# Keeping three more units on chip and loading in tiles twice as long, in a two-pass channel gate

## Chip, cores, metric

The kernel runs on one core of one Trainium2 chip. The metric is device microseconds (us) of one execution. Engines: PE multiplies matrices, DVE works on vectors, ACT applies functions such as the sigmoid, and 16 DMA engines move data between memory (HBM) and the chip's SBUF. PSUM is the small memory that PE adds up in. A packet is the piece of a transfer that the profile records for one DMA engine; here it is one contiguous run of one partition. Ratios are the mean time of one kernel's fast runs over that of the other's fast runs of the same rounds, so they are not quite the ratio of the medians that stand beside them.

## What is computed

Input `x` is 384 x 384 positions of 384 channels in bf16 (113.25 MB). The mean of each channel over all positions goes through a scale and a sigmoid; then every position is multiplied by the result.

```python
g = jnp.einsum("bhwc->bc", x) / (H * W)
s = _sigmoid(g * w1d[0])          # k = 1: cut from the padded sum over k
return x * s[:, None, None, :]
```

The gate needs all of `x` before the first output can be made, and `x` is over four times what the kernel may keep on chip (its budget is 206 KB for each of 128 partitions). So what was not kept has to be read twice.

## The kernel before

`x` is cut into 72 units of 1.573 MB: 128 partitions, 16 consecutive rows (12 KB) each. Pass 1 loads every unit and adds it up on PE, with matmuls against ones into one PSUM tile. The last 13 units stay in SBUF (`res`); the other 59 pass through four slots (`stream`). Pass 2 reads those 59 again, multiplies each in place on DVE and stores it from the ACT queue; then the 13 residents are stored.

```python
# pass 1 (set-up cut)
for t in range(n_tiles):                       # 72
    if t < n_stream:                           # 59
        xt = stream.tile([P, F], mybir.dt.bfloat16, tag="x")
    else:
        xt = res.tile([P, F], mybir.dt.bfloat16, tag="r")
        res_tiles[t] = xt
    nc.sync.dma_start(xt[:], xv[t])
    ...
    for j in range(J):                         # 16 matmuls into acc
        ...
nc.scalar.activation(s_t[:], acc[:], mybir.ActivationFunctionType.Sigmoid, scale=scale_f[:])
# pass 2
for t in range(n_stream):
    xt = stream.tile([P, F], mybir.dt.bfloat16, tag="x")
    nc.sync.dma_start(xt[:], xv[t])
    mul(xt)
    nc.scalar.dma_start(ov[t], xt[:])
for t in range(n_stream, n_tiles):
    xt = res_tiles[t]
    mul(xt)
    nc.scalar.dma_start(ov[t], xt[:])
```

## Time and profile before

| | before |
|---|---|
| time, median of the first 6 runs | 758.73 us (757.11 to 760.18) |
| busy: PE, DVE | 27%, 32% of the span |
| transfers | 131 loads and 72 stores of 1.573 MB |
| DMA rate: pass 1, pass 2, drain | 424, 428, 423 GB/s |

These are lines of the page of the kernel before. DMA and GB/s have one value for each fortieth of the span (a digit is a tenth of busy share). Then come the bytes, the multiply's group, and two DMA issue groups with count, KB each and median us from issue to landing.

```profile
DMA  8999999999999999999999999999999999999899
GB/s 335 424 426 425 423 425 424 426 424 424 426 424 424 425 423 430 427 426 432 422 425 422 429 431 422 422 427 432 425 430 429 431 430 430 432 429 430 373 426 384
...
HBM read 206.05 MB, written 113.25 MB: 422 GB/s over the span
...
L96 DVE TENSOR_TENSOR xt<-xt,s_t 128x6144 bf16<-128x6144 bf16 x72 | 240.3, 3357 | 464.9 <-ACT s_t L91 268.5
...
xt<-in_x_dram SPq DMA_DIRECT2D x131, 1536.0 KB, 12.7
out_dram<-xt ACTq DMA_DIRECT2D x72, 1536.0 KB, 12.9
```

The DMA engines are busy from the second slice to the end and nothing else is: time is bytes over rate, plus holes. One slice near the end (373) and the first and last are lower.

The windows view of the same kernel gives each engine's busy time (count) in a stretch; the last three columns are PE's clock, the DMA share and GB/s. The three rows are pass 1 (reads only), pass 2 (both directions) and the final drain (stores only).

```profile
20.00:260.00 240.00, 179.92 (x1035) 101.37 (x1035) 0.00 (x0) 0.00 (x0) 0.00 (x0) 0.99 1.01 424
300.00:690.00 390.00, 0.00 (x0) 0.00 (x0) 205.46 (x63) 0.00 (x0) 0.00 (x0) 0.50 1.01 428
718.00:752.00 34.00, 0.00 (x0) 0.00 (x0) 0.00 (x0) 0.00 (x0) 0.00 (x0) 0.50 1.00 423
```

The Trainium skill ("DMA: Bandwidth & Descriptors", section "Where 436 GB/s comes from") puts the ceiling of the 16 engines at 435.2 GB/s. This trace is 2 to 3% under it, which fits a ceiling but doesn't yet show one.

Fine windows of the same kernel show the hole near the end. The last streamed unit has been read, its multiply (the third number of a row after the length is DVE) runs, and stores behind it in the ACT queue wait.

```profile
711.00:712.50 1.50, 0.00 (x0) 0.00 (x0) 1.50 (x1) 0.00 (x0) 0.00 (x0) 0.50 0.81 344
712.50:714.00 1.50, 0.00 (x0) 0.00 (x0) 1.50 (x1) 0.00 (x0) 0.00 (x0) 0.50 0.19 82
714.00:715.50 1.50, 0.00 (x0) 0.00 (x0) 0.17 (x1) 0.00 (x0) 0.00 (x0) 0.50 0.35 147
```

At the turn between the passes there is no hole, and the timeline of the same kernel says why. The last matmuls start at 274.06 and the first multiply at 277.47, but loads into the four stream slots were queued long before and keep the engines reading until about 284.

```profile
274.06 2.76 PE L86 MATMUL acc<-xt,ones 128*128 128x384 bf16 x16 [1.98 <-DMA xt<-in_x_dram]
...
276.85 0.58 ACT L91 ACTIVATE s_t<-acc,scale_f 128x384 bf16<-128x384 f32 x1 [267.62 <-PE acc L86]
277.47 22.97 DVE L96 TENSOR_TENSOR xt<-xt,s_t 128x6144 bf16<-128x6144 bf16 x7 [268.48 <-ACT s_t L91]
```

### The profile page before, as it was taken

The page shows a single profiled execution, that of the slowest core. Times are in us where ns is not written, and L with a number is a line of the kernel's source. Part 1 is how long each engine was busy: PE and PEld are TensorE (multiplying, and loading weights), DVE is VectorE, ACT ScalarE, POOL GpSimd, SP SyncE. Part 2 cuts the span into 40 slices and gives each one's busy share as a digit, 9 for nine tenths or more (in the row PEclk, how much of TensorE's full clock was granted, in tenths as well). Part 3 has the DMA queues.
Part 4 walks back from the last instruction along what each step waited for, and adds up shares of the span by engine and source line. Part 5 has one row for each costly group of instructions (what it writes and reads, how often), then busy time and mean ns, then how long its engine had stood idle before and what let it go on. Part 6 is the DMA issues. An engine that isn't in the chain of part 4 may idle for free.

```text
span 757.5 us, 2869 instructions
## 1 busy us (share of the span) xinstructions
PE 202.0 (27%) x1152; PEld 113.5 (15%) x1152; DVE 240.6 (32%) x74; ACT 2.1 (0%) x3; POOL 0.9 (0%) x5
## 2 busy tenths in 40 slices
PE   5687777777777740000000000000000000000000
PEld 2344444444444420000000000000000000000000
DVE  0000000000000038566767563444453544535300
ACT  0000000000000000000000000000000000000000
POOL 0000000000000000000000000000000000000000
PEclk9999999999999985555555555555555555555555
DMA  8999999999999999999999999999999999999899
GB/s 335 424 426 425 423 425 424 426 424 424 426 424 424 425 423 430 427 426 432 422 425 422 429 431 422 422 427 432 425 430 429 431 430 430 432 429 430 373 426 384
DMA packets 29277, 319.48 MB, mean 422 GB/s; under 512 B 3280, under 2 KB 3280, under 8 KB 3280
## 3 DMA queue, kind: packets, MB, share of 16 engines
q1 hardware_dynamic: 18864, 206.05, 64.6%
q10 hardware_dynamic: 10368, 113.25, 35.2%
q8 instruction: 9, 0.15, 0.1%
q14 instruction: 4, 0.03, 0.0%
q0 software_dynamic: 32, 0.00, 0.0%
HBM read 206.05 MB, written 113.25 MB: 422 GB/s over the span
## 4 chain that ended last, share of the span: by engine, by line
DMA 78%; DVE 8%; PE 6%; issue 1%; SPq 0%; DVEq 0%; ACT 0%; POOLq 0%
DMA xt<-in_x_dram 53%; DMA out_dram<-xt 25%; DVE xt L96 8%; PE acc L86 6%; DMA w_b<-in_w1d_dram 1%; SPq L75 0%; DVEq L96 0%; ACT s_t L91 0%; SPq L104 0%; DVE scale_f L79 0%; POOLq L136 0%; POOLq L125 0%
## 5 line engine op out<-in xcount | busy, mean ns | idle before, releaser
L96 DVE TENSOR_TENSOR xt<-xt,s_t 128x6144 bf16<-128x6144 bf16 x72 | 240.3, 3357 | 464.9 <-ACT s_t L91 268.5
L86 PE MATMUL acc<-xt,ones 128*128 128x384 bf16 x1152 | 202.0, 330 | 74.8 <-DMA xt<-in_x_dram 65.8
L86 PEld LDWEIGHTS <-ones 128*128 128x128 bf16 x1152 | 113.5, 99 | 162.9 <-issue 93.0
L79 DVE TENSOR_SCALAR scale_f<-w_b 128x1 f32<-128x1 bf16 x1 | 0.2, 154 | 7.8 <-DMA w_b<-in_w1d_dram 7.8
L91 ACT ACTIVATE s_t<-acc,scale_f 128x384 bf16<-128x384 f32 x1 | 0.6, 581 | 267.6 <-PE acc L86 267.6
L80 ACT ACT_TABLE_LOAD x1 | 1.3, 1283 | 0.7 <-PEq L125 0.7
L78 POOL DMA_DIRECT2D w_b<-in_w1d_dram x1 | 0.7, 661 | 0.8 <-POOLq L125 0.8
L77 DVE MEMSET ones<- 128x128 bf16 x1 | 0.2, 165 | 0.8 <-PEq L125 0.8
L80 ACT ACTIVATE dummy<-scale_f 128x1 f32<-128x1 f32 x1 | 0.2, 204 | 7.0 <-DVE scale_f L79 7.0
L125 POOL MEMSET const-bfloat16-1.0<- 128x1 bf16 x1 | 0.1, 97 | 0.0
L125 POOL MEMSET const-float32-0.0<- 128x1 f32 x1 | 0.1, 94 | 0.2 <-issue 0.2
L125 POOL MEMSET const-float32-1.0<- 128x1 f32 x1 | 0.1, 94 | 0.0
L125 POOL MEMSET const-uint8-127<- 128x1 uint8 x1 | 0.1, 94 | 0.0
## 6 DMA issues: line engine op xcount, KB each, us to landing
xt<-in_x_dram SPq DMA_DIRECT2D x131, 1536.0 KB, 12.7
out_dram<-xt ACTq DMA_DIRECT2D x72, 1536.0 KB, 12.9
w_b<-in_w1d_dram POOLq DMA_DIRECT2D x1, 0.2 KB, 7.6
```

Of the source, the lines that this page charges most:

```text
L77: nc.vector.memset(ones[:], 1.0)
L78: nc.gpsimd.dma_start(w_b[:], w1d.to_broadcast((P, 1)))
L79: nc.vector.tensor_scalar_mul(scale_f[:], w_b[:], 1.0 / float(HW))
L80: nc.scalar.activation(dummy[:], scale_f[:], mybir.ActivationFunctionType.Sigmoid)
L86: nc.tensor.matmul(acc[:], lhsT=ones[:], rhs=xt[:, j * C:(j + 1) * C], start=first, stop=last,)
L91: nc.scalar.activation(s_t[:], acc[:], mybir.ActivationFunctionType.Sigmoid, scale=scale_f[:])
L96: nc.vector.tensor_mul(xt[:].rearrange("p (j c) -> p j c", j=J), xt[:].rearrange("p (j c) -> p j c", j=J), s_bc,)
L125: nc = _bacc.Bacc("TRN2", target_bir_lowering=False, num_devices=1)
```

## The change

The intent is to read three units less in pass 2, to move pass 1 in longer pieces, and to close the hole near the end:

- Two units ("kept") stay in two of the four stream slots between the passes. A third is copied by DVE into six idle PSUM banks as 32-bit words; its product is made from PSUM and stored last but one of the streamed units.
- Pass 1 loads two units at a time as 32 rows (24 KB) per partition, through six slots that later hold 12 of the 13 residents.
- Pass 2 begins with the kept units, the very first in halves, so that stores start early.

```diff
-    for t in range(n_tiles):
-        ...                                    # one unit per load, stream or res slot
+    # ---- pass 1: everything in 32-row tiles through the slots of the later residents
+    for u in range(0, N_RE - 1, 2):            # N_RE = 57
+        bt = bigs.tile([P, 2 * F], mybir.dt.bfloat16, tag="b")
+        nc.sync.dma_start(bt[:], big(xf, u))   # units u, u+1 as 32 rows per partition
+        add_up(bt, 2 * J)
+    # one unit that is read again, then the kept ones, in stream slots
+    xt = stream.tile([P, F], mybir.dt.bfloat16, tag="x")
+    nc.sync.dma_start(xt[:], xv[N_RE - 1])
+    add_up(xt, J)
+    for b in range(F // BK):                   # 6 PSUM banks
+        nc.vector.tensor_copy(keep[b][:], xt[:, b * BK:(b + 1) * BK].bitcast(mybir.dt.float32))
+    for u in range(N_RE, N_RE + KEPT):         # KEPT = 2, in stream slots
+        ...
+    for u in range(N_RE + KEPT, U - 1, 2):     # 6 big residents
+        ...
+    rt = one.tile([P, F], mybir.dt.bfloat16)   # the 13th resident, one unit
+    nc.sync.dma_start(rt[:], xv[U - 1])
+    add_up(rt, J)
     nc.scalar.activation(s_t[:], acc[:], ...Sigmoid, scale=scale_f[:])
+    for a in range(0, 1280, C):                # s_x: the gate repeated, for the PSUM banks
+        ...
+    for n, (u, xt) in enumerate(kept):
+        for a, rows in (((0, J // 2), (J // 2, J // 2)) if n == 0 else ((0, J),)):
+            mul(xt, a, rows)
+            nc.scalar.dma_start(...)
-    for t in range(n_stream):
+    order = list(range(N_RE - 2)) + [N_RE - 1, N_RE - 2]   # the unit in PSUM last but one
+    for u in order:
         ...
+        if u == N_RE - 1:
+            for b in range(F // BK):
+                nc.vector.tensor_mul(xt[:, ...], keep[b][:].bitcast(mybir.dt.bfloat16), s_x[:, o:o + BK])
```

More of the change, by code (lines that the diff above doesn't have):

```diff
@@ L6 @@
 from concourse._compat import with_exitstack
-J_TARGET = 16
-STREAM_BUFS = 4
-SBUF_BUDGET_KB = 206.0
-MIN_TILES_PER_PASS = 4
-def _plan(HW, C, P, jt=None, sbufs=None, budget=None):
-    jt = J_TARGET if jt is None else jt
-    sbufs = STREAM_BUFS if sbufs is None else sbufs
-    budget = SBUF_BUDGET_KB if budget is None else budget
-    rows_per_part = HW // P
-    divs = [d for d in range(1, rows_per_part + 1) if rows_per_part % d == 0]
-    J = 1
-    for cand in divs:
-        if cand <= jt and rows_per_part // cand >= MIN_TILES_PER_PASS:
-            J = cand
-    n_tiles = rows_per_part // J
-    F = J * C
-    tile_kb = F * 2 / 1024.0
-    avail = budget - 1.0 - sbufs * tile_kb
-    R = int(avail // tile_kb) if avail > 0 else 0
-    R = max(0, min(R, n_tiles - sbufs - 1))
-    return J, n_tiles, F, R
 @with_exitstack
@@ L44 @@
     HW = B * H * W
-    assert HW % P == 0
-    assert C <= 512
-    J, n_tiles, F, R = _plan(HW, C, P)
-    n_stream = n_tiles - R
+    J = 16
+    F = J * C
+    U = HW // (P * J)
+    N_BIG, KEPT, BUFS = 6, 2, 4
+    RES = 2 * N_BIG + 1
+    N_RE = U - RES - KEPT
     xf = x.rearrange("b h w c -> (b h w) c")
@@ L53, with big @@
     ov = of.rearrange("(n p j) c -> n p (j c)", p=P, j=J)
+    def big(ap, u):
+        rows = ap[u * P * J:(u + 2) * P * J, :]
+        return rows.rearrange("(p j) c -> p (j c)", p=P, j=2 * J)
     consts = ctx.enter_context(tc.tile_pool(name="consts", bufs=1))
-    stream = ctx.enter_context(tc.tile_pool(name="stream", bufs=STREAM_BUFS))
-    res = ctx.enter_context(tc.tile_pool(name="res", bufs=max(R, 1)))
+    stream = ctx.enter_context(tc.tile_pool(name="stream", bufs=BUFS))
+    bigs = ctx.enter_context(tc.tile_pool(name="bigs", bufs=N_BIG))
+    one = ctx.enter_context(tc.tile_pool(name="one", bufs=1))
     psum = ctx.enter_context(tc.tile_pool(name="psum", bufs=1, space=bass.MemoryType.PSUM))
@@ L65, with add_up @@
     s_t = consts.tile([P, C], mybir.dt.bfloat16)
-    s_bc = s_t[:].unsqueeze(1).to_broadcast((P, J, C))
-    res_tiles = {}
-    for t in range(n_tiles):
-        if t < n_stream:
-            xt = stream.tile([P, F], mybir.dt.bfloat16, tag="x")
-        else:
-            xt = res.tile([P, F], mybir.dt.bfloat16, tag="r")
-            res_tiles[t] = xt
-        nc.sync.dma_start(xt[:], xv[t])
-        if t == 0:
+    BK = 1024
+    keep = [psum.tile([P, BK // 2], mybir.dt.float32, name=f"keep{b}", tag=f"keep{b}") for b in range(F // BK)]
+    s_x = consts.tile([P, 1280], mybir.dt.bfloat16)
+    done = [0]
+    def add_up(xt, rows):
+        for j in range(rows):
+            nc.tensor.matmul(
+                acc[:], lhsT=ones[:], rhs=xt[:, j * C:(j + 1) * C],
+                start=(done[0] == 0), stop=(done[0] == U * J - 1),
+            )
+            done[0] += 1
+    for u in range(0, N_RE - 1, 2):
+        bt = bigs.tile([P, 2 * F], mybir.dt.bfloat16, tag="b")
+        nc.sync.dma_start(bt[:], big(xf, u))
+        if u == 0:
             nc.vector.memset(ones[:], 1.0)
@@ L82 @@
             )
-        for j in range(J):
-            first = (t == 0 and j == 0)
-            last = (t == n_tiles - 1 and j == J - 1)
-            nc.tensor.matmul(
-                acc[:], lhsT=ones[:], rhs=xt[:, j * C:(j + 1) * C],
-                start=first, stop=last,
-            )
+        add_up(bt, 2 * J)
[4 more added lines that the diff above has]
+        nc.vector.tensor_copy(keep[b][:], xt[:, b * BK:(b + 1) * BK].bitcast(mybir.dt.float32))
+    kept = []
+    for u in range(N_RE, N_RE + KEPT):
+        xt = stream.tile([P, F], mybir.dt.bfloat16, tag="x")
+        nc.sync.dma_start(xt[:], xv[u])
+        add_up(xt, J)
+        kept.append((u, xt))
+    res = []
+    for u in range(N_RE + KEPT, U - 1, 2):
+        bt = bigs.tile([P, 2 * F], mybir.dt.bfloat16, tag="b")
+        nc.sync.dma_start(bt[:], big(xf, u))
+        add_up(bt, 2 * J)
+        res.append((u, bt))
+    rt = one.tile([P, F], mybir.dt.bfloat16)
+    nc.sync.dma_start(rt[:], xv[U - 1])
+    add_up(rt, J)
     nc.scalar.activation(
@@ L93, with mul @@
     )
-    def mul(xt):
-        nc.vector.tensor_mul(
-            xt[:].rearrange("p (j c) -> p j c", j=J),
-            xt[:].rearrange("p (j c) -> p j c", j=J),
-            s_bc,
-        )
-    for t in range(n_stream):
-        xt = stream.tile([P, F], mybir.dt.bfloat16, tag="x")
-        nc.sync.dma_start(xt[:], xv[t])
-        mul(xt)
-        nc.scalar.dma_start(ov[t], xt[:])
-    for t in range(n_stream, n_tiles):
-        xt = res_tiles[t]
-        mul(xt)
-        nc.scalar.dma_start(ov[t], xt[:])
+    for a in range(0, 1280, C):
+        n = min(C, 1280 - a)
+        nc.scalar.activation(
+            s_x[:, a:a + n], acc[:, :n], mybir.ActivationFunctionType.Sigmoid, scale=scale_f[:]
+        )
+    def mul(t, a, rows):
+        v = t[:, a * C:(a + rows) * C].rearrange("p (j c) -> p j c", j=rows)
+        nc.vector.tensor_mul(v, v, s_t[:].unsqueeze(1).to_broadcast((P, rows, C)))
+    for n, (u, xt) in enumerate(kept):
+        for a, rows in (((0, J // 2), (J // 2, J // 2)) if n == 0 else ((0, J),)):
+            mul(xt, a, rows)
+            nc.scalar.dma_start(ov[u][:, a * C:(a + rows) * C], xt[:, a * C:(a + rows) * C])
+    order = list(range(N_RE - 2)) + [N_RE - 1, N_RE - 2]
+    for u in order:
+        xt = stream.tile([P, F], mybir.dt.bfloat16, tag="x")
+        if u == N_RE - 1:
+            for b in range(F // BK):
+                o = b * BK % C
+                nc.vector.tensor_mul(
+                    xt[:, b * BK:(b + 1) * BK], keep[b][:].bitcast(mybir.dt.bfloat16), s_x[:, o:o + BK]
+                )
+        else:
+            nc.sync.dma_start(xt[:], xv[u])
+            mul(xt, 0, J)
+        nc.scalar.dma_start(ov[u], xt[:])
+    for u, bt in res:
+        for h in range(2):
+            mul(bt, h * J, J)
+            nc.scalar.dma_start(big(of, u)[:, h * F:(h + 1) * F], bt[:, h * F:(h + 1) * F])
+    mul(rt, 0, J)
+    nc.scalar.dma_start(ov[U - 1], rt[:])
 _INS = ['x', 'w1d']
```

## The prediction

> **What bounds the kernel now.** The 16 DMA engines. The page's 40 slices show them at a share of 0.9 or more from the second slice on, while PE is busy 27% of the span and DVE 32%. The page counts 206.05 MB read and 113.25 MB written: 72 units of 1.573 MB read once, 59 read again, 72 written, 203 transfers. The windows view gives 424 GB/s in pass 1 (20 to 260 us, reads only), 428 in pass 2 (300 to 690) and 423 in the final drain (718 to 752, writes only): 3.71, 3.67 and 3.72 us a unit. The Trainium skill, page "DMA: Bandwidth & Descriptors", section "Where 436 GB/s comes from", puts the ceiling at 435.2 GB/s; the trace is within 3% of it, so little but fewer bytes can help.
>
> Time not at that rate, from windows of 1 to 1.5 us: about 4 us at the start; nothing at the turn between the passes (four stream slots read ahead); about 2.3 us at 711 to 715.5, where the last streamed read has landed and its multiply (3.36 us) must end before its store and the resident stores queued behind it can go; about 2 us after the last byte.
>
> **What the change does, and its cost.**
> 1. Two units stay in stream slots between the passes and one stays in PSUM: 56 units are read again, not 59. Three transfers less at 3.68 us: -11.0 us, all on the critical path.
> 2. The unit from PSUM is stored while the last read is in flight, so the hole at 711 to 715 should nearly close: -2 us.
> 3. Pass 1 loads 3.1 MB at a time, 24 KB per partition rather than 12. Single-direction phases run 1% slower than pass 2, perhaps from what each packet or transfer costs; half of that over 72 units: -1.5 us (an estimate, 0 to -3).
> 4. The turn: two slots read ahead (7.4 us) instead of four. After the last landing come 2.8 us of matmuls, 0.6 us sigmoid, half a multiply (1.7 us) and about 0.9 us to the first stored byte; the reads ahead just cover this, but the second kept unit's multiply ends about 1.3 us after the stores before it, and four extra sigmoids (0.6 us each or less) sit in the ACT queue before the first store: +1.6 us.
> 5. Copies to PSUM, and the product from PSUM. The skill, page "VectorE: DVE Perf Modes", section "The perf-mode tier table", gives tensor_tensor with a PSUM operand 1x, so I estimate 7 us instead of 3.36 for that unit; no record of before shows it. DVE has slack (one read and one write take 7.35 us): off the path.
>
> **Predicted:** 758.7 - 11.0 - 2.0 - 1.5 + 1.6 = 745.8 us (ratio 0.983), 8 in 10 between 742.5 and 749.5. Faster by over 2% (under 743.6): 0.19; within 2%: 0.80; slower: 0.01.
>
> **What would show each step.** (1) 201.3 MB read; 56 second reads in the issue list. (2) No slice below 400 GB/s near the end except the last. (3) Rate of pass 1 against 424. (4) In fine windows, the DMA share at the turn. (5) DVE records of the PSUM product around 1.1 us for each 1024 values; nobody waiting on it.
>
> **What would make it wrong.** 24 KB runs raising (or lowering) the rate by more than 1%: each 1% of pass 1 is 2.7 us, the likeliest way to pass 2%. A longer hole at the turn, if two slots cover less than I reckon or the ACT queue holds stores back. Pass 2 starved after the turn (second reads wait for stores of kept units). A hole left at the end if the PSUM product delays the last multiply.

## The result

The changed kernel takes 748.05 us (median of 8 runs, 747.25 to 749.28), the kernel before 758.59 us (16 runs). The ratio is 0.9861, with a 95% interval of 0.9849 to 0.9874. That is 1.4% faster: "within 2%", and inside the predicted range.

The same lines of the page after the change, with the copies to PSUM (L79) and the products from PSUM (L120) in place of the multiply's group:

```profile
DMA  8999999999999989999999999999999999999998
GB/s 340 428 431 427 428 433 426 433 428 428 431 426 428 431 372 365 432 429 429 430 432 428 428 431 431 428 429 431 430 430 428 433 429 430 429 433 420 414 431 375
...
HBM read 201.33 MB, written 113.25 MB: 422 GB/s over the span
...
L79 DVE COPY keep<-xt 128x512 f32<-128x512 f32 x6 | 3.7, 686 | 204.7 <-DMA xt<-in_x_dram 204.7
...
L120 DVE TENSOR_TENSOR xt<-keep,s_x 128x1024 bf16<-128x1024 bf16 x6 | 3.8, 682 | 0.0
...
bt<-in_x_dram SPq DMA_DIRECT2D x34, 3072.0 KB, 38.4
xt<-in_x_dram SPq DMA_DIRECT2D x59, 1536.0 KB, 13.2
```

Three things are to be seen. 201.33 MB is read, 4.72 MB less. Pass 1 slices stand near 429 instead of 424. And the mean over the span is still 422 GB/s, because two slices in the middle (372 and 365, the turn) are new, while the 373 near the end has gone to 414.

The windows view of the changed kernel confirms the rates:

```profile
20.00:260.00 240.00, 183.70 (x1045) 104.95 (x1045) 3.66 (x6) 0.00 (x0) 0.00 (x0) 0.96 1.00 429
300.00:680.00 380.00, 0.00 (x0) 0.00 (x0) 210.19 (x63) 0.00 (x0) 0.00 (x0) 0.50 1.01 430
```

Fine windows of the changed kernel at the turn (rows left out are full):

```profile
272.50:274.00 1.50, 1.50 (x11) 0.90 (x10) 0.00 (x0) 0.00 (x0) 0.00 (x0) 1.00 1.03 434
274.00:275.50 1.50, 0.53 (x4) 0.10 (x1) 0.32 (x1) 0.93 (x2) 0.00 (x0) 1.00 0.87 369
275.50:277.00 1.50, 0.00 (x0) 0.00 (x0) 1.50 (x2) 1.32 (x4) 0.00 (x0) 1.00 0.31 131
277.00:278.50 1.50, 0.00 (x0) 0.00 (x0) 1.50 (x1) 0.00 (x0) 0.00 (x0) 1.00 0.50 205
...
281.50:283.00 1.50, 0.00 (x0) 0.00 (x0) 1.50 (x2) 0.00 (x0) 0.00 (x0) 0.50 0.40 160
...
284.50:286.00 1.50, 0.00 (x0) 0.00 (x0) 1.50 (x2) 0.00 (x0) 0.00 (x0) 0.50 1.17 319
286.00:287.50 1.50, 0.00 (x0) 0.00 (x0) 1.50 (x1) 0.00 (x0) 0.00 (x0) 0.50 0.88 295
```

And the timeline of the changed kernel there (start, us, engine, line, operation, tiles, count, idle before and its releaser):

```profile
266.57 5.36 PE L56 MATMUL acc<-bt,ones 128*128 128x384 bf16 x32 [1.97 <-DMA bt<-in_x_dram]
...
271.77 2.76 PE L56 MATMUL acc<-rt,ones 128*128 128x384 bf16 x16
274.57 0.58 ACT L96 ACTIVATE s_t<-acc,scale_f 128x384 bf16<-128x384 f32 x1 [263.75 <-PE acc L56]
275.05 1.78 ACT L101 ACTIVATE s_x<-acc,scale_f 128x384 bf16<-128x384 f32 x4
275.18 13.23 DVE L107 TENSOR_TENSOR xt<-xt,s_t 128x3072 bf16<-128x3072 bf16 x5 [56.25 <-ACT s_t L96]
276.97 5.28 ACTq L113 DMA_DIRECT2D out_dram<-xt  x3
```

There are three separate losses at the turn: (a) from 274 to 277.5, nothing left to read and nothing yet to store; (b) at 281.5 to 283, where the second kept unit's multiply was not done when the two half stores were out; (c) from 284.5 to about 290, where the engines count as busy (share 0.88 to 1.17) but move only 280 to 420 GB/s. (The view counts a packet where it starts, so a share can pass 1.)

To size all this I worked out, from the packet records of each trace, how many bytes each stretch moved (a packet's bytes spread evenly over its time) and compared that with 430 GB/s. The difference is time lost. "Start" is the first 20 us and "pass 1" goes from there to the turn. "Turn a, b, c" are the stretches from 7 us before the first stored byte to 1 after it, 1 to 6 after, and 6 to 15 after; "end" is 75 to 30 us before the last byte, "drain" the last 30 us.

```
us lost        start  pass 1  turn a   b     c    pass 2   end   drain
before          3.9    3.7     0.1    0.0   0.0    2.3     2.6    0.4
changed         4.1    0.8     2.0    1.2   1.6    0.2     1.0    0.9
  again (e11)   3.7    0.8     2.8    1.2   1.8    0.3     1.3    0.7
```

The bytes are worth 4.72 MB / 430 GB/s = 11.0 us. Pass 1 gains 2.9, the turn costs 4.7 (5.7 in the second trace), the end gains 1.6 (1.3). The kernel before lost 2.3 us in the middle of pass 2 in stretched packets; there is one trace of it, so I don't know whether that is usual. The two profiled spans (757.5 and 745.0) differ by 12.5 us, more than the medians' 10.5: the profiled execution of the kernel before took 759.25 us, 0.7 above its median, and that of the changed kernel 746.88, 1.2 below.

### The profile page after: what moved, and what is told of

Read it like the earlier page. It is cut to its first block, busy times and chain, and to the rows that moved or that the text cites. A ratio compares the mean times of both kernels' runs of the same rounds, so it can differ in the third digit from the quotient of the medians.

```text
span 745.0 us, 2819 instructions
## 1 busy us (share of the span) xinstructions
PE 203.1 (27%) x1152; PEld 115.9 (16%) x1152; DVE 244.6 (33%) x86; ACT 3.7 (1%) x7; POOL 0.9 (0%) x5
## 3 DMA queue, kind: packets, MB, share of 16 engines
q1 hardware_dynamic: 13536, 201.33, 63.6%
HBM read 201.33 MB, written 113.25 MB: 422 GB/s over the span
## 4 chain that ended last, share of the span: by engine, by line
DMA 79%; DVE 8%; PE 5%; issue 2%; SPq 0%; ACT 0%; DVEq 0%
DMA bt<-in_x_dram 32%; DMA out_dram<-xt 25%; DMA xt<-in_x_dram 22%; DVE xt L107 7%; PE acc L56 5%; SPq L65 0%; DVE xt L120 0%; ACT s_t L96 0%; DVEq L107 0%; SPq L124 0%; DVE bt L107 0%
## 5 line engine op out<-in xcount | busy, mean ns | idle before, releaser
L107 DVE TENSOR_TENSOR xt<-xt,s_t 128x6144 bf16<-128x6144 bf16 (+1 forms) x59 | 194.6, 3303 | 237.2 <-DMA xt<-in_x_dram 170.6
L56 PE MATMUL acc<-bt,ones 128*128 128x384 bf16 x1088 | 192.5, 338 | 70.9 <-DMA bt<-in_x_dram 70.9
L56 PEld LDWEIGHTS <-ones 128*128 128x128 bf16 x1152 | 115.9, 101 | 158.2 <-issue 88.7
L79 DVE COPY keep<-xt 128x512 f32<-128x512 f32 x6 | 3.7, 686 | 204.7 <-DMA xt<-in_x_dram 204.7
L107 DVE TENSOR_TENSOR bt<-bt,s_t 128x6144 bf16<-128x6144 bf16 x12 | 40.1, 3352 | 0.0
L56 PE MATMUL acc<-xt,ones 128*128 128x384 bf16 x48 | 8.1, 326 | 0.5 <-DMA xt<-in_x_dram 0.5
L120 DVE TENSOR_TENSOR xt<-keep,s_x 128x1024 bf16<-128x1024 bf16 x6 | 3.8, 682 | 0.0
L107 DVE TENSOR_TENSOR rt<-rt,s_t 128x6144 bf16<-128x6144 bf16 x1 | 3.4, 3352 | 0.0
L56 PE MATMUL acc<-rt,ones 128*128 128x384 bf16 x16 | 2.8, 326 | 0.0
L101 ACT ACTIVATE s_x<-acc,scale_f 128x384 bf16<-128x384 f32 (+1 forms) x4 | 1.8, 533 | 0.0
## 6 DMA issues: line engine op xcount, KB each, us to landing
out_dram<-xt ACTq DMA_DIRECT2D x58, 1536.0 KB, 12.5
```

The lines of the kernel that those rows point to most:

```text
L56: nc.tensor.matmul(acc[:], lhsT=ones[:], rhs=xt[:, j * C:(j + 1) * C], start=(done[0] == 0), stop=(done[0] == U * J - 1),)
L79: nc.vector.tensor_copy(keep[b][:], xt[:, b * BK:(b + 1) * BK].bitcast(mybir.dt.float32))
L101: nc.scalar.activation(s_x[:, a:a + n], acc[:, :n], mybir.ActivationFunctionType.Sigmoid, scale=scale_f[:])
L107: nc.vector.tensor_mul(v, v, s_t[:].unsqueeze(1).to_broadcast((P, rows, C)))
L120: nc.vector.tensor_mul(xt[:, b * BK:(b + 1) * BK], keep[b][:].bitcast(mybir.dt.bfloat16), s_x[:, o:o + BK])
```

## Experiments

All variants start from the changed kernel. "a, b, c" and "lost" have the meaning above. All gave correct results.

### Why is pass 1 faster: layout, size of the transfer, or length of the run?

Theory A is that each packet has a fixed cost, so 24 KB packets beat 12 KB ones. Rival B is the distance in HBM between what the engines move at once (24 KB instead of 12). A third possibility is the size of the transfer as such (3.1 MB instead of 1.57). Two variants go back to 12 KB runs; e1 keeps the layout and e2 the size of the transfer.

e1_halves: same layout, half the transfer, runs of 12 KB.

```diff
-        nc.sync.dma_start(bt[:], big(xf, u))
+        for h in range(2):
+            nc.sync.dma_start(bt[:, h * F:(h + 1) * F], big(xf, u)[:, h * F:(h + 1) * F])
```

> Each 3.1 MB load of pass 1 (not of the residents) is split into two of 1.57 MB: runs of 12 KB per partition, but still 32 consecutive rows per partition, so the partitions are 24 KB apart in HBM. Question: why does pass 1 run at 429 GB/s after the change and at 424 before? Theory A (the prediction's step 3: fewer, longer packets or transfers): pass 1 falls back to 424 GB/s, packets of 12 KB take 466 ns, the kernel is about 2.9 us slower than the changed one (ratio to before 0.990). Rival B (the distance in HBM between what the 16 engines move at once; the drain's stores also went from 423 to 429 with packets of unchanged size): pass 1 stays at 429 GB/s, packets take 460 ns, ratio stays 0.986. The turn is not touched: its hole stays near 3 us either way.

e2_12k_runs: whole 3.1 MB transfers, the old layout (for the residents' stores too), runs of 12 KB.

```diff
-        return rows.rearrange("(p j) c -> p (j c)", p=P, j=2 * J)
+        return rows.rearrange("(n p j) c -> p n (j c)", n=2, p=P, j=J)
```

> Still one 3.1 MB transfer for each pair of units, but laid out as before the change: 16 consecutive rows per partition from each of the two units, so 256 packets of 12 KB and partitions 12 KB apart; stores of the residents in the same layout. If transfers of 3.1 MB as such were the gain: pass 1 at 429 GB/s. If packet length (A) or the distance in HBM (B) is: 424. B alone also says that the final drain of the residents falls back from 429 to 423 GB/s; A leaves it at 429 (stores were packets of 12 KB all along). Ratio to before: 0.986 if transfer size, about 0.990 to 0.991 otherwise.

Measured: e1 750.08 us (ratio 0.9881), e2 751.70 us (0.9902). Windows of pass 1, of e1 (whose last 38 us there are residents still loaded in 24 KB runs) and of e2:

```profile
20.00:260.00 240.00, 178.32 (x1024) 100.51 (x1023) 3.66 (x6) 0.00 (x0) 0.00 (x0) 0.99 1.01 426
```

```profile
20.00:260.00 240.00, 186.05 (x1043) 105.58 (x1041) 3.66 (x6) 0.00 (x0) 0.00 (x0) 0.95 1.01 425
```

Both fall back to the rate of before or near it; the time lost in pass 1 is 3.1 us in e1 and 3.5 in e2, against 3.7 before and 0.8 changed. So neither the layout nor the transfer size is enough for the gain. (As a time, e1 lies between what the two theories expected, and its interval overlaps the changed kernel's; the rate decides.) In e1 packets of both lengths run in one trace: 12 KB take 466.1 ns on average, 24 KB 917.3 ns. Theory A holds. Rival B had been suggested to me by the drain (423 GB/s before, 429 changed); but e1, whose stores are exactly those of the changed kernel, drained with packets of 465 ns, so the drain's rate varies from trace to trace for another reason, which stays open.

Fitting 12 KB and 24 KB in one direction gives 14.8 ns for each packet and 451.2 ns for each 12 KB. The second number is 27.2 bytes per ns, times 16 engines 435.7 GB/s: the skill's ceiling of 435.2, nearly to the digit. The 6 KB packets of the half stores took 238 ns at the median in the changed kernel, where the fit says 240. e9_quads tests the fit at 48 KB:

```diff
-    N_BIG, KEPT, BUFS = 6, 2, 4
+    N_BIG, KEPT, BUFS = 3, 2, 4          # three slots of four units, 64 rows per partition
...
+        for a, n in (((0, 2), (2, 1), (3, 1)) if u == U - 1 - Q else ((0, Q),)):
+            nc.sync.dma_start(bt[:, a * F:(a + n) * F], big(xf, u)[:, a * F:(a + n) * F])
```

> The changed kernel with tiles of four units: three slots of 48 KB per partition, loads of 6.3 MB in packets of 48 KB; the last of them in three pieces (two units, one, one) so that the sum is not late. The packet times read so far fit 14.8 ns + 451.2 ns for each 12 KB (12 KB alone in one direction 466.0, 24 KB 917.2, 6 KB 241). Theory (a fixed cost for each packet): 48 KB take 1820 ns, pass 1 runs at 432 GB/s, 1.7 us gained over the changed kernel: 746.3. Rival (24 KB is where it ends, or three slots are too coarse): packets longer than 1835 ns or waits of the load queue, 748 us or more.

Measured: packets of 48 KB take 1821.5 ns (fit: 1819.6), and the few of 24 KB, here with partitions 48 KB apart, still 916.5. The windows view of e9, for pass 1 and for a part of it in which all packets are of 48 KB:

```profile
20.00:260.00 240.00, 191.79 (x1060) 109.14 (x1060) 3.66 (x6) 0.00 (x0) 0.00 (x0) 0.92 1.00 430
40.00:200.00 160.00, 125.71 (x697) 71.53 (x696) 0.00 (x0) 0.00 (x0) 0.00 (x0) 0.91 1.00 432
```

In that part the changed kernel moves 429 and the kernel before 424 GB/s, so the fit holds at 432. All of pass 1, which also has single units, loses 1.1 us less than in the changed kernel. Yet the time did not fall: 748.51 us (0.9869), against 748.88 (0.9868) for the changed kernel. The gain was given back: in the traces the turn lost 6.6 us against 5.8 in the control, in piece (a) (taken apart below), and the end 2.3 against 1.3.

### The three units alone

e3_singles keeps the kept units, PSUM and all orders, but loads single units into 13 single slots.

```diff
-    bigs = ctx.enter_context(tc.tile_pool(name="bigs", bufs=N_BIG))
+    bigs = ctx.enter_context(tc.tile_pool(name="bigs", bufs=RES))     # RES = 13 single units
...
-        nc.sync.dma_start(bt[:], big(xf, u))
+        nc.sync.dma_start(bt[:], xv[u])
```

> The change without its 3.1 MB tiles: 13 resident slots of one unit each, all loads 1.57 MB in the layout of before; the kept units, the unit in PSUM and all orders stay. So only the three transfers fewer and the end are left. The prediction's own sum gives 758.6 - 11.0 - 2.0 + 1.6 = 747.2. Theory T (the changed kernel's turn is held up by the coarse 3.1 MB loads: after the last big one lands PE still has 32 + 16 matmuls = 8.1 us to do, where the last single unit would need 2.8 us after its landing): last landing to first store byte shortens by about 1.5 us, pass 1 and the drain go back to 424 and 423 GB/s (+3.5 us): about 750 us, ratio 0.989. Rival (the hole at the turn is only due to having two slots to read ahead instead of four): the hole stays at 2 us before the first store byte, and the time is about 751.5, ratio 0.991.

Measured: 751.91 us (0.9905). It lost 3.7 us in pass 1 and 1.8, 1.2 and 1.7 us in the three pieces of the turn. So the turn's loss is there without any big tile: it comes with the kept units. The rival's time (751.5) fits; theory T, that big loads make most of the hole, does not, although the next section shows that they have a share in it.

### What the turn's loss is made of

e4_last_halves splits only the last 3.1 MB load.

```diff
+        if u == U - 3:
+            for h in range(2):
+                nc.sync.dma_start(bt[:, h * F:(h + 1) * F], big(xf, u)[:, h * F:(h + 1) * F])
+        else:
             nc.sync.dma_start(bt[:], big(xf, u))
```

> Only the last 3.1 MB load before the final unit is split into two loads of 1.57 MB (same rows per partition), so that PE can start on its first half 3.7 us earlier. Theory T (coarse last load delays the end of the sum): PE is done 1.3 to 1.5 us sooner relative to the last byte read, the hole before the first store shrinks from about 2 us to 0.5 us, pass 1 stays at 429 GB/s, time about 746.6, ratio 0.984. Rival (two slots of read-ahead are too few in any case, PE is not late): hole and time unchanged, ratio 0.986.

Measured: 747.06 us (0.9844, interval 0.9824 to 0.9864, overlapping the changed kernel's). That is near the time which theory T expected (746.6), but the hole before the first store only shrank from 2.0 to 1.5 us. In its timeline PE now waits for the last load instead of being behind:

```profile
271.34 2.76 PE L56 MATMUL acc<-rt,ones 128*128 128x384 bf16 x16 [1.35 <-DMA rt<-in_x_dram]
```

In the changed kernel (timeline above) the last 16 matmuls followed the 32 before them without a gap. So the coarse last load did make PE late, yet the start of the last matmuls moved only from 271.77 to 271.34. What PE waits for explains the rest. In the packet records the 16 completions of one load, one for each DMA engine, do not come together. Those of `rt` spread over 2.4 us in the changed kernel and 3.7 in e4 (269.4 and 270.4 us for the last), and those of the last load before the hole end between 274.5 and 277.3 in the changed kernel. The Trainium skill ("DMA: Bandwidth & Descriptors", section "Why a DMA increments its semaphore by 16 and not by 1") says that the engines of a transfer finish independently and that only the full 16 means everything has landed; the trace agrees. The sum must wait for the slowest engine, while the fastest runs out of read-ahead up to about 3 us before that one does. My prediction had treated the 16 engines as one.

The semaphore updates of `rt` take (a) apart in every trace. "PE late" is how long after the last engine of `rt` has reported the last matmuls start; "slowest" is how long after the mean of the 16 that engine reports.

```
us             changed   e11   e1   e2   e3   e4   e6   e7   e9   e12
PE late           1.55  1.55 1.55 3.23 0.04 0.04 3.22 1.54 0.89  1.55
slowest           1.22  1.95 0.99 1.25 2.45 2.08 1.13 1.62 3.55  1.35
piece (a)          2.0   2.8  1.8  3.7  1.8  1.5  3.5  2.4  3.7   2.2
```

In all ten traces with two slots of read-ahead and 16 matmuls after the last load (in e3, of the last unit loaded), (a) is the sum of the two less 0.6 to 0.9 us. So splitting the last load saved 1.5 us of lateness in e4, and an engine that came 0.9 us later in that trace hid more than half of it. In e9 the lateness was less than in the changed kernel; the wait for the slowest engine was the larger part. What makes the engines of one load drift apart, no run here shows: e10, with the same four-unit loads, had them closer together.

PE was twice as late in e2 and e6 for a reason that their edits don't touch. During the 32 matmuls before the last 16, the clock granted to PE fell to half for some 3 us, so they took 7.04 us instead of 5.36. Timeline and window of e6:

```profile
266.31 7.04 PE L56 MATMUL acc<-bt,ones 128*128 128x384 bf16 x32 [1.96 <-DMA bt<-in_x_dram]
```

```profile
267.00:270.40 3.40, 3.40 (x12) 1.58 (x11) 0.00 (x0) 0.00 (x0) 0.00 (x0) 0.50 1.02 424
```

In the changed kernel's trace the same window has PE's clock at 1.00. Earlier in pass 1 PE has time to spare (it waited 1.8 to 2.0 us for each of the last big loads), but here the sum waits for it.

e5_kept1 gives one slot back to the read-ahead and reads one unit more.

```diff
-    N_BIG, KEPT, BUFS = 6, 2, 4
+    N_BIG, KEPT, BUFS = 6, 1, 4          # and one more single unit in pass 1
```

> The changed kernel with one kept unit instead of two: 57 second reads instead of 56 (+3.67 us of transfer), but three stream slots to read ahead at the turn instead of two. The trace of the changed kernel loses about 5 us at the turn against 430 GB/s, in three pieces: 2.0 us before the first store byte (the 16 DMA engines run dry at times spread over 2.9 us while the sum waits for the slowest of them), 1.1 us when the second kept unit's multiply is late, 1.6 us of stretched packets while second reads restart. Theory (read-ahead is what the kept slots cost): the loss at the turn falls to 0.5 to 1.5 us, so the time is within 0.7 us of the changed kernel's, 747.5 to 748.5: the second kept unit bought almost nothing. Rival (the loss comes from the two-pass structure and the extra operations, not from the slots): the loss stays near 5 us and the time rises by 3.7 to about 751.7.

Measured: 749.30 us (0.9876). The turn loses 0.4 + 0.8 + 1.7 = 2.9 us. Piece (a) is nearly gone, although this trace has the slow clock too and PE was 3.2 us late: the third slot covered what two would not have. So (a) is a matter of read-ahead; the rival, a loss near 5 us, is out. But (c) stays, which I had not expected, so the time is above the theory's 747.5 to 748.5. Against the changed kernel (748.05) the second kept unit, worth 3.7 us in bytes, brings about 1.2 us, and the intervals of the two ratios overlap.

e6_kept2_halves stores the second kept unit in halves too.

```diff
-        for a, rows in (((0, J // 2), (J // 2, J // 2)) if n == 0 else ((0, J),)):
+        for a, rows in ((0, J // 2), (J // 2, J // 2)):
```

> The second kept unit is multiplied and stored in halves like the first. Theory: the dip in the DMA share at 281 to 283 us comes from its multiply ending after the stores before it are out; with halves the first of its bytes is ready 1.7 us earlier and this piece (1.1 us) vanishes, the other two stay: 747 us, ratio 0.985. Rival (the dip is the second reads waiting for the slot of the first kept unit): the dip stays or moves, 748 us.

Measured: 747.70 us (0.9853). Piece (b) falls from 1.2 to 0.4 us, so (b) is the late multiply. Piece (a) was 3.5 us in this profiled run, which the edit doesn't touch: the slow clock above.

e8_turn shortens the whole chain from the last landing to the first store.

```diff
+    for a in (0, F // 2):                      # very last unit in two loads
+        nc.sync.dma_start(rt[:, a:a + F // 2], xv[U - 1][:, a:a + F // 2])
-        for a, rows in (((0, J // 2), (J // 2, J // 2)) if n == 0 else ((0, J),)):
+        for a, rows in ((0, 4), (4, 4), (8, 8)) if n == 0 else ((0, 8), (8, 8)):
```

(and the split of e4.)

> A version made for the turn: last 3.1 MB load split in two units, the very last unit loaded in two halves (so that only 8 matmuls, 1.4 us, follow the last landing), first kept unit multiplied in a quarter, a quarter and a half, second in halves. If the hole before the first store is only the length of the chain from last landing to first store (theory), that chain shortens from 5.7 to about 3.5 us, the first two pieces of the loss (2.0 + 1.1 us) vanish and the third stays: about 745, ratio 0.982. Rival (packets of 6 and 3 KB and the spread of the engines eat the gain): 747 to 748.

Measured: 746.19 us (0.9843, interval 0.9812 to 0.9875). The turn in windows of e8, where the share in the changed kernel had fallen to 0.31:

```profile
273.00:274.50 1.50, 0.13 (x1) 0.00 (x0) 0.72 (x1) 1.33 (x3) 0.00 (x0) 1.00 0.97 410
274.50:276.00 1.50, 0.00 (x0) 0.00 (x0) 1.50 (x3) 0.92 (x3) 0.00 (x0) 0.98 0.85 350
276.00:277.50 1.50, 0.00 (x0) 0.00 (x0) 1.50 (x2) 0.00 (x0) 0.00 (x0) 0.50 0.90 365
```

Pieces (a) and (b) are 0.4 us each, (c) is 2.1. The time lies between theory (745) and rival (747 to 748); this trace lost 2.0 us at the end, where the changed kernel lost 1.0. So (a) is the length of the chain against two slots of read-ahead, (b) is the late multiply, and (c) is neither. Piece (c) was 1.6 to 2.1 us in the traces of the changed kernel and of all twelve variants, and 0.0 in the kernel before, whose second reads never stopped. In these traces it comes when second reads start again after stores alone; why 12 KB packets then take up to 1.0 us in the changed kernel (1.56 in e8) instead of 0.46 no run here shows.

### The hole near the end

e7_psum_mid, and e12_psum_mid_again with more rounds, store the PSUM unit in the middle of pass 2. e11_after_again is the control.

```diff
-    order = list(range(N_RE - 2)) + [N_RE - 1, N_RE - 2]   # the unit in PSUM last but one
+    order = list(range(28)) + [N_RE - 1] + list(range(28, N_RE - 1))
```

> The unit held in PSUM is stored after 28 units of pass 2, not last but one. Bytes are the same. Theory (the prediction's step 2: its place covers the multiply of the last streamed read): the hole near the end comes back, loss between 670 and 720 us rises from about 1.0 to about 2.5 us, time +1.5 us: 749.5, ratio 0.988. Rival (the hole had closed for another reason, such as the order in which the stores of the residents are issued): no change, 748.

> The same kernel as the one that stores the PSUM unit in the middle of pass 2, with more rounds, beside the control. Its first trace lost only 1.2 us between its last reads and the drain, against 1.0 for the changed kernel and 2.6 for the kernel before, but its time was 1.5 us over the changed kernel's with a wide interval. If the place last but one is worth the 2 us of the prediction's step 2: 2 us slower than the control. If it is worth only what the traces say: 0 to 0.5 us slower.

> The changed kernel unchanged, as the control beside the other runs of this call: 748.0, ratio 0.986; and whether the pieces of loss in its first trace (turn 4.9 us, end 1.0 us, pass 1 0.7 us) come back in a second trace.

Measured: e7 749.62 us (0.9884, interval 0.9851 to 0.9916); e12 748.56 us (0.9875) beside the control's 748.88 us (0.9868). The ratios differ by 0.0007, 0.5 us, well inside their intervals; the medians by less, and the other way. The same window, first of e12, then of the control:

```profile
698.50:700.00 1.50, 0.00 (x0) 0.00 (x0) 1.04 (x1) 0.00 (x0) 0.00 (x0) 0.50 0.21 90
```

```profile
698.50:700.00 1.50, 0.00 (x0) 0.00 (x0) 0.06 (x1) 0.00 (x0) 0.00 (x0) 0.50 0.95 401
```

So the hole does come back when the PSUM unit is moved: the mechanism is right. In the 6 us after the last read's end 2.4 us were lost before, 0.0 and 0.1 in the changed kernel and its control, 1.0 in e7 and 1.5 in e12. But the order with the PSUM unit last but one pays about 1 us of this in another coin: its last read then runs alone, after stores alone, at 328 to 369 GB/s instead of 430 (686 to 692 us in the changed kernel). By the table's measure the end loses 1.0 and 1.3 us with it last but one, and 1.2 and 1.8 with it in the middle, where the middle also loses about 0.8 us more. The place doesn't always close the hole: the end lost 3.1, 2.3 and 2.0 us in e1, e9 and e8, whose edits don't touch it, and 1.4, 0.7 and 0.8 of that came after the last read. e7's time, taken alone, was the 749.5 that its theory expected; e12 with its control did not repeat it. The place is worth between nothing clear and 1 us, not 2.

### All together

e10_all takes the four-unit tiles, the early stores, the last unit in two loads and the PSUM unit in the middle, stores one resident just before the last streamed unit, and loads `w1d` from the ACT queue.

```diff
-            nc.gpsimd.dma_start(w_b[:], w1d.to_broadcast((P, 1)))
+            nc.scalar.dma_start(w_b[:], w1d.to_broadcast((P, 1)))
...
+        if u == order[-1]:
+            mul(rt, 0, J)
+            nc.scalar.dma_start(ov[U - 1], rt[:])
```

> All that helped, and two more: tiles of four units; the last loads in pieces down to half a unit; first kept unit multiplied in quarter, quarter and half, second in halves; the unit in PSUM stored in the middle of pass 2; one resident multiplied and stored just before the last streamed unit, so that its multiply is covered; w1d loaded through the ACT queue rather than by GpSimd. Summing the pieces against the changed kernel: packets -1.7, turn -1.9, end -0.5 to -1; if the GpSimd load causes the dip of the DMA share at 5 to 8 us (about 2 us lost), -2 more. Theory with the dip due to that load: 741.5, ratio 0.978. Rival (the dip belongs to the first transfers): 743.5, ratio 0.980.

Measured: 746.65 us (0.9848), against 748.88 us (0.9868) for the control. Both expectations were too good. The start lost 4.1 us as always, so GpSimd's load of `w1d` is not its cause. Piece (a) was 2.5 us, not 0.4: in its timeline the last 16 matmuls ran without a gap from 271.48, behind those of the four-unit tile, 128 matmuls without a gap. The end lost 1.9 us, 1.6 of it after the last read, so the resident stored just before the last streamed unit didn't cover that unit's multiply. The best versions, e8 (746.19) and e10 (746.65), have the lowest medians of all, some 2 us under the changed kernel, but their intervals overlap its interval, and by ratio e4 (0.9844) is as low.

The pieces of all variants, in us lost:

```
               start  pass 1  turn a   b     c    pass 2   end   drain
e1_halves       4.0    3.1     1.8    1.2   1.9    0.3     3.1    0.4
e2_12k_runs     4.1    3.5     3.7    1.2   1.9    0.3     1.5    1.2
e3_singles      4.1    3.7     1.8    1.2   1.7    0.2     1.4    1.1
e4_last_halves  4.1    1.0     1.5    1.2   1.9    0.2     0.9    0.8
e5_kept1        3.6    0.9     0.4    0.8   1.7    0.7     1.8    1.2
e6_kept2_halves 3.7    0.9     3.5    0.4   1.8    0.1     1.2    1.0
e7_psum_mid     3.9    0.8     2.4    1.2   1.8    1.0     1.2    0.4
e8_turn         4.1    1.0     0.4    0.4   2.1    0.2     2.0    1.2
e9_quads        4.2   -0.3     3.7    1.2   1.7    0.3     2.3    0.9
e10_all         4.1   -0.3     2.5    0.8   1.6    1.0     1.9    0.5
e12 (as e7)     3.7    0.8     2.2    1.2   1.9    1.1     1.8    0.4
```

## Why the prediction was right, point by point

The direction, the range (742.5 to 749.5) and the class were right, and the bound was right: DMA time, so bytes over rate. Two of its terms were mis-sized by a factor of two or more, in opposite directions.

1. Bytes, "-11.0 us": right. 4.72 MB less at 430 GB/s is 11.0 us, and 56 units are read again: 59 loads into `xt` in the issue list, less the three of pass 1.
2. End, "-2 us": too large. The slice of 373 became 414, and the hole does return when the PSUM unit is moved away, but the last read, alone after stores alone, now loses about 1 us that it did not lose before. The end gained 1.6 us in one trace and 1.3 in the other, and the two orders differ by no more than 1 us.
3. Longer loads, "-1.5 us (an estimate, 0 to -3)": right in kind, too small. Pass 1 gained 2.9 us, and e1, e2 and e9 show that the length of a run makes it.
4. Turn, "+1.6 us": the term that was most off; it measured 4.7 and 5.7. "The reads ahead just cover this" failed: read-ahead ends when the fastest engine has nothing left, while the sum waits for the slowest, about 3 us apart (the last engine of `rt` 1.2 us after the mean), and the last 3.1 MB load put PE 1.55 us behind, where the sum had only 2.8 us of matmuls after the last landing. The late second multiply was right (1.2 us against 1.3). The extra sigmoids in the ACT queue cost nothing: they end at 276.83, before the first store could be issued at 276.97. And piece (c), 1.6 to 2.1 us, was not in the sum at all.
5. PSUM: off the path, as said. But the product took 3.8 us (six of 682 ns, which overlap a little), not 7.

With the terms of the first trace the sum is -11.0 - 1.6 - 2.9 + 4.7 = -10.8, and with those of the second -11.0 - 1.3 - 2.9 + 5.7 = -9.5; measured are -10.5 and predicted were -12.9. That the prediction came out near is partly luck: step 3 gained 1.4 us more than it said, step 4 cost 3 to 4 us more.

## What to carry to other kernels

A buffer that is kept full across a phase change is a buffer less for read-ahead; price it by what the DMA engines will do while the first result is being made, not by the bytes it saves. Count read-ahead from the engine that finishes first and the wait from the one that finishes last, and make the last loads before a global reduction small, the first products after it small too. In a DMA-bound stage, longer contiguous runs per packet still pay at 12 KB, but only as long as the coarser tile does not delay the consumer at the end of the stage.

## What the Trainium skill lacked or had wrong

- "DMA: Bandwidth & Descriptors", section "Why small descriptors are slow (HBM only)": it puts a fixed overhead of about 3 cycles on a packet, and says combining them is only worth it up to 256 bytes. In these traces the fixed part is 14.8 ns per packet record (466 ns for 12 KB, 917 for 24, 1821.5 for 48), so going from 12 to 24 KB runs raised a reads-only stage from 424 to 429 GB/s. Whether it is the same overhead, no run shows.
- Same page, section "Rules for kernel authors": it asks for at least 1 MiB per DMA. Here 3.1 MB transfers with 12 KB runs were no faster than 1.57 MB ones (425 against 424 GB/s in pass 1); above that size it was run length that counted.
- Same page: no number for how far apart the engines of one transfer finish. Here the completions of the last 1.57 MB load before the sum, in a full queue, spread over 1.7 to 5.5 us (e1, e9).
- Same page: nothing on the slow restart of reads after a stretch of stores alone. 12 KB packets took up to 1.0 us (1.56 in e8) instead of 0.46 for some microseconds, 1.6 to 2.1 us lost each time; the cause is open.
- "VectorE: DVE Perf Modes", section "The perf-mode tier table": it gives tensor_tensor with any PSUM operand 1x. Here bf16 products with one operand in PSUM took 682 ns for 1024 values per partition. That is no slower than from SBUF: the multiplies in e8 (954, 1751 and 3358 ns for 1536, 3072 and 6144 values) put 687 ns on the same line. A later section of the page, "Why PSUM operands drop a tier", allows 2x_1P, and that is what the runs fit.
